# First layer's steady blocks: two steps' first products in one PSUM bank, activations 512 columns wide

## The chip, the cores and the metric

The kernel runs on one core of one Trainium2 chip. The metric is the device time of a whole execution in microseconds. The median before is 1391.65 us over three runs (1391.5 to 1392.34).

## The reference

Three computations run one after the other on 4608 tokens of width 512 (8 batches of 576):

```
attention: chunks of 64 tokens, 8 heads of 64; softmax(q k^T / 8) v within a chunk
first layer:  h = x @ w_in (512 x 2048);  g = h * sigmoid(h);  x = g @ w_out (2048 x 512)
experts:  logits = x @ w_gate + modality_bias[modality_id];  e = argmax
          out = softmax(logits)[e] * (max(x @ w1[e], 0) @ w2[e])   w1[e] 512 x 1024, w2[e] 1024 x 512
```

## The kernel before, in words

Every matrix operand is kept as a high and a low part, and a product is three matmuls: high by high, high by low, low by high. The first layer works on blocks of 256 tokens, `j` = 0 to 17. Blocks 0 and 1 run as a pair while weights are still converted (`order_of`, `g_pair`, lines 136 to 199 and 623 to 644), with activations that are up to 512 columns wide, one half for each block. The change leaves them alone. Blocks 2 to 17 are the steady blocks, the loop from line 1293 on.

A steady block has 16 steps of work, one for each 128 columns of the hidden width, and two more to drain (`NF` = 16, `LAG` = 2). Step `st` does this, in the order in which it is issued:

- `g_parts(j, st - 1)`: ScalarE casts the activation of the step before to its high part (line 653), VectorE subtracts for the low part (line 655).
- Side work: the attention of the next block's two token tiles, router work from a list, woven together by `weave` (one piece of each in turn).
- `g1(j, st)`: the first products, 12 matmuls of 256 columns into one PSUM tile (line 609); then tanh on ScalarE (line 617) and a fused add and multiply on VectorE (line 618), both 256 columns wide. PSUM tile `psh` has two buffers, each one bank of 512 columns; half of a bank is used.
- More side work, then `finish_step(j, st)`: the second products of step `st - 2`, six matmuls of 512 columns into two accumulators (lines 668 to 670). After the last of them the accumulators are copied out, stored, and the block's router work is put on the list.

Each engine runs its instructions in the order of issue. A block has 36 places for side work, two a step. The lists `EVEN` and `ODD` (lines 37 and 38) give, for a block's even and odd attention tile, the places of five pieces: query transpose (VectorE, line 370), scores (TensorE, with maximum, subtract and exponential behind them), normalisation (VectorE), transpose of the probabilities (TensorE), and the product with the values. The key transpose (line 377) comes two places after the query transpose. A negative place lies in the block before. The loads of the next tile are issued by SP with the scores and with the transpose of the probabilities; SP works through its own queue and runs ahead.

Router work: `pump` takes one or two entries of the list a step, first 16 dot products of 512 columns on VectorE (line 690), then `route`, some dozen tiny operations; `pump_late` starts `place` (five tiny matmuls, then small VectorE work and two scatters) one step after `route` at the earliest (`due`, line 1211). In the last block the side places also hold the index gathers and index copies of the first expert tiles (lines 1298 and 1299), their transposes (`trans_x`, lines 1302 and 1303) and the loading and splitting of the first expert's weights.

The expert layer that follows works in stages of two steps: 24 first products of 256 columns (line 1099), each step's relu for itself, then 12 second products of 512 columns (lines 1125 to 1127).

Of the kernel before, what the change touches and what calls it, by code (L numbers as in the profile page):

```python
# [9 lines left out]
F32 = mybir.dt.float32  # L10
# [4 lines left out]
ACTF = mybir.ActivationFunctionType  # L15
ALU = mybir.AluOpType
# [4 lines left out]
P = 128  # L21
# [12 lines left out]
BLK32 = 3  # L34


EVEN = (-12, -8, 5, 9, 15)
ODD = (9, 15, 19, 24, 28)
EVEN0 = (3, 9, 11, 15, 20)
ODD0 = (15, 20, 22, 26, 30)  # L40

# [161 lines left out]
def attention_moe_moe_kernel(  # L203
# [14 lines left out]
    nc = tc.nc  # L218
# [6 lines left out]
    NF = DFF // P  # L225
# [4 lines left out]
    scale = 1.0 / float(D) ** 0.5  # L230

    const = ctx.enter_context(tc.tile_pool(name="const", bufs=1))
    sb = ctx.enter_context(tc.tile_pool(name="sb", bufs=1))
# [29 lines left out]
    def ps_h():  # L263
        return ps.tile([P, 512], F32, tag="h", bufs=2, name="psh")
# [320 lines left out]
    def weave(gens):  # L585

        gens = list(gens)
        while gens:
            gens = [g for g in gens if next(g, weave) is not weave]


    gst = {}

    gps = {}

    def g1(j, f):
        g1_mm(j, f)
        g1_act(j, f)

    def g1_mm(j, f, pair=None):  # L600
        half, fi = divmod(f, 8)
        hi, lo = xT[j]
        hps = ps_h() if pair is None else pair
        n = 0
        for kk in range(KD):
            wh = big1[:, half * 4 + kk, 0, fi * P:(fi + 1) * P]
            wl = big1[:, half * 4 + kk, 1, fi * P:(fi + 1) * P]
            for w, x in ((wh, hi), (wh, lo), (wl, hi)):
                nc.tensor.matmul(hps[:, :256], lhsT=w, rhs=x[:, kk, :], start=n == 0, stop=n == 3 * KD - 1)  # L609
                n += 1  # L610
        if pair is None:
            gps[j, f] = hps

    def g1_act(j, f):
        hps = gps.pop((j, f))
        g = sb.tile([P, 256], F32, tag="g", bufs=3, name="g")
        nc.scalar.activation(out=g, in_=hps[:, :256], func=ACTF.Tanh, scale=0.5)  # L617
        nc.vector.scalar_tensor_tensor(out=g, in0=g, scalar=1.0, in1=hps[:, :256], op0=ALU.add, op1=ALU.mult)  # L618
        gst[j, f] = g

    pair = {}

# [23 lines left out]
    def hid(name, shape):  # L646
        return sb.tile(shape, F32R, tag="hid", bufs=5, name=name)

    def g_parts(j, f):
        g = gst[j, f]  # L650
        gx = hid("g", [P, 2, 256])
        gh, gl = gx[:, 0], gx[:, 1]
        nc.scalar.copy(gh, g)  # L653
        yield
        nc.vector.tensor_tensor(out=gl, in0=g, in1=gh.bitcast(F32), op=ALU.subtract)  # L655
        gst[j, f] = (gh, gl)

    acc = {}

    def g2(j, f):  # L660
        gh, gl = gst.pop((j, f))
        half, fi = divmod(f, 8)
        pc, o = half * 4 + fi // 2, (fi % 2) * 512
        wh, wl = big2[:, pc, 0, o:o + 512], big2[:, pc, 1, o:o + 512]
        for t in range(2):
            c = slice(t * P, (t + 1) * P)
            a = acc[j][t]
            nc.tensor.matmul(a, lhsT=gh[:, c], rhs=wh, start=f == 0, stop=False)  # L668
            nc.tensor.matmul(a, lhsT=gh[:, c], rhs=wl, start=False, stop=False)  # L669
            nc.tensor.matmul(a, lhsT=gl[:, c], rhs=wh, start=False, stop=f == NF - 1)  # L670
# [4 lines left out]
    def x2_evac(j):  # L675
        x2[j] = []
        for t in range(2):
            x = t2("x2t")
            nc.scalar.activation(out=x, in_=acc[j][t], func=ACTF.Copy, scale=0.5)  # L679
            r0 = (2 * j + t) * P  # L680
            nc.sync.dma_start(out=x2d[r0:r0 + P, :], in_=x)
            x2[j].append(x)
        del acc[j]
        if j < NB - 1:
            lg[j] = sb.tile([P, 2, E], F32, tag="lg", bufs=2, name="lg")
# [482 lines left out]
    with tc.manual_schedule():  # L1168
# [3 lines left out]
        def once(fn, *a):  # L1172
            fn(*a)
            return
            yield
# [7 lines left out]
        def att_side(side, t, steps):  # L1183
            fns = (att_Tq, att_S, att_norm, att_PT32, att_PV32)
            side[steps[0] + 2].append(lambda: att_Tk(t))
            for fn, f in zip(fns, steps):
                one = fn in (att_Tq, att_PT32)
                side[f].append((lambda fn=fn: once(fn, t)) if one else (lambda fn=fn: fn(t)))
            if t + 1 < NTILE:
                side[steps[1]].append(lambda: once(load_qk, t + 1))  # L1190
                side[steps[3]].append(lambda: once(load_nat, t + 1, "v"))

        rq = []
        now, due = [0], [0]

        def push_router(j):
            for i in range(2 * E):
                rq.append(("d", lambda i=i: once(dot, j, i)))
            rq.append(("r", lambda: route(j)))
            rq.append(("p", lambda: place(j, *pend.pop(j))))  # L1200
            if j == NB - 3:
                rq.append(("r", choose_first))

        def pump(n):
            out = []
            while wg and rq and n > 0 and rq[0][0] != "p":
                kind, fn = rq.pop(0)
                out.append(fn())
                n -= 1
                if kind != "d":  # L1210
                    due[0] = now[0] + 1
                    break
            return out

        def pump_late():
            if rq and rq[0][0] == "p" and now[0] >= due[0]:
                g = rq.pop(0)[1]()
                next(g)
                return [g]
            return []  # L1220

        def finish_step(j, st):
            f = st - LAG
            if 0 <= f < NF:
                if f == 0:
                    mk = ps_att if j == 1 else ps_acc
                    acc[j] = [mk(), mk()]
                g2(j, f)
                if f == NF - 1:
                    x2_evac(j)  # L1230
                    if j < NB - 1:
                        push_router(j)
# [4 lines left out]
        for n, idle in todo:  # L1237
            what = n[0]
            hps = None
            if what == "g1":  # L1240
                st = n[2] + n[1] * SKEW
# [3 lines left out]
                hps = gps[st][:, n[1] * 256:(n[1] + 1) * 256]  # L1245
# [16 lines left out]
            if n == ("lo", NF - 1):  # L1262
# [7 lines left out]
                    out=wgb.rearrange("p e d -> p (e d)"),  # L1270
                    in_=wgt_d.rearrange("(o e) d -> o (e d)", o=1).to_broadcast([P, E * DM]),
# [14 lines left out]
        late_gens = []  # L1286
        nsteps = NF + LAG
        sides = {i: [] for i in range(2 * nsteps * (NB - 2))}
        for t in range(2 * BLK32, NTILE):
            base = 2 * nsteps * (t // 2 - BLK32)  # L1290
            steps = (ODD if base else ODD0) if t % 2 else (EVEN if base else EVEN0)
            att_side(sides, t, [base + i for i in steps])
        for j in range(2, NB):
            last = j == NB - 1
            side = {i: sides.pop(2 * nsteps * (j - 2) + i) for i in range(2 * nsteps)}
            if last:
                for i in range(2 * FIXED):
                    side[8].append(lambda i=i: once(gather_id, i))
                    side[12].append(lambda i=i: once(make_oid, i))
                side[14].append(lambda: once(gather, 0))  # L1300
                side[14].append(lambda: once(gather, 1))
                side[26].append(lambda: once(trans_x, 0))
                side[30].append(lambda: once(trans_x, 1))
                for n in range(8):
                    i, h = divmod(n, 2)
                    side[(8, 9, 16, 17, 20, 21, 24, 25)[n]].append(lambda i=i, h=h: once(load_first, i, h))
                    f1, f2 = ((8, 10), (9, 11), (12, 13), (14, 15))[i]
                    side[2 * f1 + h].append(lambda i=i, h=h: split_first(i, 0, h))
                    side[2 * f2 + h].append(lambda i=i, h=h: split_first(i, 1, h))
            for st in range(nsteps):  # L1310
                now[0] += 1
                gens = [g_parts(j, st - 1)] if 1 <= st <= NF else []
                gens += [fn() for fn in side[2 * st]] + late_gens
                if j > 2 or st > 1:
                    gens += pump(2 if last or len(rq) > 16 else 1)
                weave(gens)
                if st < NF:
                    g1(j, st)
                weave([fn() for fn in side[2 * st + 1]])
                finish_step(j, st)  # L1320
                late_gens = pump_late()
        assert not rq
        j = NB - 1

# [76 lines left out]
        last = 2 * LONE  # L1401
# [95 lines left out]
```

## Time and profile before

| | |
|---|---|
| median of three runs | 1391.65 us |
| the profiled execution | 1393.78 us |
| its span, first to last instruction | 1392.0 us |
| mean granted clock of TensorE over the span | 0.995 |
| busy: TensorE, VectorE, ScalarE, GpSimd | 98%, 69%, 44%, 12% |
| steady blocks | from 137.4 us to 941.4 us |

In the profile PE is TensorE's matmul, PEld its weight loads, DVE VectorE, ACT ScalarE, POOL GpSimd and SP SyncE, which issues DMAs. A matmul's start is recorded and its end is modelled, so the distance from start to start says how fast the stream runs. A part in square brackets at the end of a timeline row is the idle time before that instruction and what released it. Granted clock 1.00 is the full 2.4 GHz.

### The profile page before, as it was taken

What the parts mean: (1) busy time and instruction counts of PE and PEld (TensorE: products, weight loads), DVE (VectorE), ACT (ScalarE), POOL (GpSimd) and SP (SyncE); (2) the same over time, 40 slices, a digit from 0 to 9 for tenths busy, and PEclk for the clock granted to TensorE, in tenths of its full rate; (3) what the DMA queues carried; (4) which work ended last, traced back from release to release, by engine and by line L of the source; (5) the groups of instructions that cost most, each with busy time, mean ns of one, the idle gap of its engine ahead of it and who ended that gap; (6) DMA issues with size and microseconds to landing.
All of it is one profiled execution on the core that took longest, in us unless ns stands there. A gap on an engine that the chain in (4) does not pass through costs nothing. (4 is left out here: it accounts for less than half of the span.)

```text
span 1392.0 us, 26469 instructions
## 1 busy us (share of the span) xinstructions
PE 1368.0 (98%) x9755; PEld 1226.0 (88%) x9755; DVE 967.3 (69%) x2370; ACT 606.5 (44%) x1234; POOL 160.4 (12%) x173
## 2 busy tenths in 40 slices
PE   8899999999999999999999999999999999999997
PEld 7788888988898888898898888889889989989996
DVE  5997986776777677677677767674677666666664
ACT  5554333333333333333333333352555555555553
POOL 0000000000000000000000000022223222232311
PEclk9899999999999999999999999999999999999999
DMA  9555421221131132132132120231777767776662
GB/s 214 167 177 162 102 51 35 39 59 35 31 62 31 32 62 43 20 61 50 27 47 57 32 35 24 69 85 47 245 251 217 230 208 236 212 230 223 229 208 75
DMA packets 242394, 153.81 MB, mean 110 GB/s; under 512 B 189474, under 2 KB 189510, under 8 KB 242128
## 3 DMA queue, kind: packets, MB, share of 16 engines
q1 hardware_dynamic: 234000, 133.07, 36.3%
q0 software_dynamic: 8256, 18.96, 3.7%
q8 instruction: 79, 1.29, 0.4%
q14 instruction: 59, 0.48, 0.1%
HBM read 132.48 MB, written 20.01 MB: 110 GB/s over the span
## 5 line engine op out<-in xcount | busy, mean ns | idle before, releaser
L609 PE MATMUL psh<-xh,big 128*128 128x256 f32 x2304 | 456.1, 283 | 0.0
L609 PEld LDWEIGHTS psh<-xh,big 128*128 128x128 f32 x2304 | 372.0, 189 | 12.3 <-issue 2.7
L609 PE MATMUL psh<-xl,big 128*128 128x256 f32 x1152 | 324.4, 282 | 0.1
L609 PEld LDWEIGHTS psh<-xl,big 128*128 128x128 f32 x1152 | 217.6, 189 | 9.3 <-DVE xl L526 0.3
L1099 PE MATMUL psh<-xgh,big 128*128 128x256 f32 x1152 | 217.5, 282 | 1.1 <-DVE h L1109 1.0
L618 DVE SCALAR_TENSOR_TENSOR g<-g,psh 128x256 f32<-128x256 f32 x256 | 107.1, 418 | 143.4 <-ACT g L617 140.6
L668 PE MATMUL psc<-big,g 128*128 128x512 f32 x512 | 204.7, 400 | 0.0
L670 PE MATMUL psc<-big,g 128*128 128x512 f32 x512 | 202.1, 395 | 1.3 <-DVE g L655 1.3
L669 PE MATMUL psc<-big,g 128*128 128x512 f32 x512 | 202.1, 395 | 0.0
L690 DVE CUSTOM_DVE_ANT_0 dump<-x2t,wgb 128x512 bf16<-128x512 f32 x272 | 184.9, 680 | 8.2 <-ACT x2t L679 6.3
L617 ACT ACTIVATE g<-psh 128x256 f32<-128x256 f32 x256 | 98.0, 383 | 211.0 <-PE psh L609 196.8
L1099 PEld LDWEIGHTS psh<-xgh,big 128*128 128x128 f32 x1152 | 181.7, 189 | 5.1 <-DVE h L1109 1.4
L653 ACT CAST g<-g 128x256 fp32r<-128x256 f32 x256 | 103.9, 406 | 153.4 <-DVE g L618 148.5
L1099 PE MATMUL psh<-xgl,big 128*128 128x256 f32 x576 | 161.9, 281 | 0.2 <-DVE xgl L1090 0.2
L1109 DVE SCALAR_TENSOR_TENSOR h<-psh,h 128x256 fp32r<-128x256 f32 x144 | 60.7, 423 | 127.2 <-ACT h L1108 118.2
L1108 ACT ACTIVATE h<-psh 128x256 fp32r<-128x256 f32 x144 | 55.2, 384 | 189.0 <-PE psh L1099 164.6
L787 POOL DMA_INDIRECT perm<-rpg,rdi x36 | 36.8, 1022 | 764.5 <-DVE rdi L786 638.7
L655 DVE TENSOR_TENSOR g<-g 128x256 fp32r<-128x256 f32 x256 | 107.7, 421 | 18.1 <-ACT g L653 18.1
L670 PEld LDWEIGHTS psc<-big,g 128*128 128x128 f32 x512 | 96.0, 188 | 23.8 <-DVE g L655 1.7
L1099 PEld LDWEIGHTS psh<-xgl,big 128*128 128x128 f32 x576 | 108.7, 189 | 3.8 <-DVE xgl L1090 0.5
L668 PEld LDWEIGHTS psc<-big,g 128*128 128x128 f32 x512 | 96.6, 189 | 14.9 <-ACT xh L445 2.4
L669 PEld LDWEIGHTS psc<-big,g 128*128 128x128 f32 x512 | 96.2, 188 | 12.5
(252 smaller groups left out, 2042.8 us busy)
## 6 DMA issues: line engine op xcount, KB each, us to landing
rb<-in_moe_w_dram SPq DMA_DIRECT2D x144, 256.0 KB
wr<-in_moe_w_dram SPq DMA_DIRECT2D x68, 512.0 KB
x2d<-x2t SPq DMA_DIRECT2D x36, 256.0 KB
ra<-in_moe_w_in_dram SPq DMA_DIRECT2D x8, 1024.0 KB
rb<-in_moe_w_out_dram SPq DMA_DIRECT2D x8, 1024.0 KB
qk<-in_q_dram SPq DMA_DIRECT2D x240, 32.0 KB
qk<-in_k_dram SPq DMA_DIRECT2D x240, 32.0 KB
vn<-in_v_dram SPq DMA_DIRECT2D x28, 256.0 KB
```

The costliest lines, as they stand in the source:

```text
L609: nc.tensor.matmul(hps[:, :256], lhsT=w, rhs=x[:, kk, :], start=n == 0, stop=n == 3 * KD - 1)
L617: nc.scalar.activation(out=g, in_=hps[:, :256], func=ACTF.Tanh, scale=0.5)
L618: nc.vector.scalar_tensor_tensor(out=g, in0=g, scalar=1.0, in1=hps[:, :256], op0=ALU.add, op1=ALU.mult)
L653: nc.scalar.copy(gh, g)
L655: nc.vector.tensor_tensor(out=gl, in0=g, in1=gh.bitcast(F32), op=ALU.subtract)
L668: nc.tensor.matmul(a, lhsT=gh[:, c], rhs=wh, start=f == 0, stop=False)
L669: nc.tensor.matmul(a, lhsT=gh[:, c], rhs=wl, start=False, stop=False)
L670: nc.tensor.matmul(a, lhsT=gl[:, c], rhs=wh, start=False, stop=f == NF - 1)
L690: nc.vector.tensor_tensor_reduce(out=dump, in0=x2[j][t], in1=wg[0][:, e, :], scale=1.0, scalar=0.0, op0=ALU.mult, op1=ALU.add, accum_out=l ...
L1099: nc.tensor.matmul(hp[:, :256], lhsT=w[:, part, :], rhs=x[:, :, kk * P:(kk + 1) * P], start=i == 0, stop=i == 3 * KD - 1,)
L1108: nc.scalar.activation(out=gh, in_=hp[:, :256], func=ACTF.Relu)
L1109: nc.vector.scalar_tensor_tensor(out=gl, in0=hp[:, :256], scalar=0.0, in1=gh.bitcast(F32), op0=ALU.max, op1=ALU.subtract)
```

## The change

Two steps become one stage `d`. In its first half: side work, the 12 first products of step 2d into the left half of a bank, side work, the 12 of step 2d+1 into the right half, then one tanh and one fused multiply over all 512 columns. In its second half: one cast and one subtract of 512 columns (`g_parts(j, d)`, issued in the same stage as the first products), side work, the second products of step 2d-2, side work, those of step 2d-1. Ninth stage: only the second products of steps 14 and 15. The 36 places are kept, four a stage. The high and low parts are now two tiles of 512 columns instead of the halves of one. Even tiles' query transposes move from place -12 to -15, the normalisations one place earlier, and `place` waits one step longer after `route`.

```diff
-EVEN = (-12, -8, 5, 9, 15)
-ODD = (9, 15, 19, 24, 28)
+EVEN = (-15, -8, 4, 9, 15)
+ODD = (9, 15, 18, 24, 28)
...
+    def g1_stage(j, d, side):
+
+        hps = ps_h()
+        g1_mm(j, 2 * d, hps[:, :256])
+        weave(side)
+        g1_mm(j, 2 * d + 1, hps[:, 256:])
+        pair["g", d] = g = sb.tile([P, 512], F32, tag="g", bufs=3, name="g")
+        nc.scalar.activation(out=g, in_=hps, func=ACTF.Tanh, scale=0.5)
+        nc.vector.scalar_tensor_tensor(out=g, in0=g, scalar=1.0, in1=hps, op0=ALU.add, op1=ALU.mult)
+
+    def g_parts(j, d):
+        g = pair.pop(("g", d))
+        gh, gl = hid("gh", [P, 512]), hid("gl", [P, 512])
+        nc.scalar.copy(gh, g)
         yield
         nc.vector.tensor_tensor(out=gl, in0=g, in1=gh.bitcast(F32), op=ALU.subtract)
-        gst[j, f] = (gh, gl)
+        for n in range(2):
+            gst[j, 2 * d + n] = (gh[:, n * 256:(n + 1) * 256], gl[:, n * 256:(n + 1) * 256])
...
-                    due[0] = now[0] + 1
+                    due[0] = now[0] + 2
...
-            for st in range(nsteps):
-                now[0] += 1
-                gens = [g_parts(j, st - 1)] if 1 <= st <= NF else []
-                gens += [fn() for fn in side[2 * st]] + late_gens
-                if j > 2 or st > 1:
-                    gens += pump(2 if last or len(rq) > 16 else 1)
-                weave(gens)
-                if st < NF:
-                    g1(j, st)
-                weave([fn() for fn in side[2 * st + 1]])
-                finish_step(j, st)
-                late_gens = pump_late()
+            for d in range(nsteps // 2):
+                for half in range(2):
+                    now[0] += 1
+                    gens = [g_parts(j, d)] if half and d < NF // 2 else []
+                    gens += [fn() for fn in side[4 * d + 2 * half]] + late_gens
+                    if j > 2 or d > 0:
+                        gens += pump(2 if last or len(rq) > 16 else 1)
+                    weave(gens)
+                    between = [fn() for fn in side[4 * d + 2 * half + 1]]
+                    if not half and d < NF // 2:
+                        g1_stage(j, d, between)
+                    elif not half:
+                        weave(between)
+                    else:
+                        finish_step(j, 2 * d)
+                        weave(between)
+                        finish_step(j, 2 * d + 1)
+                    late_gens = pump_late()
```

## Rows read from the trace of the kernel before

**Rows 1.** page, part 1, whole span: busy us (share) xinstructions:
```profile
PE 1368.0 (98%) x9755; PEld 1226.0 (88%) x9755; DVE 967.3 (69%) x2370; ACT 606.5 (44%) x1234; POOL 160.4 (12%) x173
```

**Rows 2.** windows of one block's length: stretch, length, busy us and count by engine, clock:
```profile
139.00:189.20 50.20, 50.16 (x370) 44.03 (x369) 44.02 (x123) 17.82 (x43) 2.12 (x2) 1.00 0.33 72
390.00:440.20 50.20, 50.20 (x371) 44.84 (x370) 35.89 (x105) 18.51 (x43) 1.92 (x2) 1.00 0.22 43
892.00:942.20 50.20, 48.89 (x317) 43.71 (x316) 36.71 (x108) 24.02 (x55) 10.82 (x10) 1.00 0.41 106
```

**Rows 3.** timeline, TensorE, first and first after two plain steps: start us, us, engine, line:
```profile
416.10 0.28 PE L609 MATMUL psh<-xh,big 128*128 128x256 f32 x1
...
421.73 0.28 PE L609 MATMUL psh<-xh,big 128*128 128x256 f32 x1
```

**Rows 4.** timeline, TensorE, two stages of the expert layer:
```profile
1157.98 0.28 PE L1099 MATMUL psh<-xgh,big 128*128 128x256 f32 x1
...
1160.83 0.40 PE L1125 MATMUL psc<-big,h 128*128 128x512 f32 x1
...
1163.63 0.28 PE L1099 MATMUL psh<-xgh,big 128*128 128x256 f32 x1
...
1169.27 0.28 PE L1099 MATMUL psh<-xgh,big 128*128 128x256 f32 x1
```

**Rows 5.** groups by line and shape, steady blocks: busy us, mean ns | idle:
```profile
L655 DVE TENSOR_TENSOR g<-g 128x256 fp32r<-128x256 f32 x256 | 107.7, 421 | 18.1 <-ACT g L653 18.1
L618 DVE SCALAR_TENSOR_TENSOR g<-g,psh 128x256 f32<-128x256 f32 x255 | 106.7, 418 | 139.9 <-ACT g L617 137.1
L653 ACT CAST g<-g 128x256 fp32r<-128x256 f32 x256 | 103.9, 406 | 153.4 <-DVE g L618 148.5 <-DVE g L655 4.4
L617 ACT ACTIVATE g<-psh 128x256 f32<-128x256 f32 x255 | 97.6, 383 | 210.1 <-PE psh L609 195.9 <-issue 9.1 <-PE psa L771 0.9
```

**Rows 6.** groups by line and shape, the paired blocks before them:
```profile
L641 DVE TENSOR_TENSOR gpl<-gp,gph 128x512 fp32r<-128x512 f32 x14 | 9.6, 684 | 0.7 <-ACT gph L638 0.7
L633 DVE SCALAR_TENSOR_TENSOR gp<-gp,psh 128x512 f32<-128x512 f32 x14 | 9.5, 678 | 0.0
...
L638 ACT CAST gph<-gp 128x512 fp32r<-128x512 f32 x14 | 8.6, 613 | 0.8 <-DVE gp L633 0.8
L629 ACT ACTIVATE gp<-psh 128x512 f32<-128x512 f32 x14 | 8.3, 594 | 3.2 <-PE psh L609 3.2
```

**Rows 7.** timeline, all engines, hand-overs after one step's first products:
```profile
404.05 0.29 PE L609 MATMUL psh<-xh,big 128*128 128x256 f32 x1
...
404.44 0.38 ACT L617 ACTIVATE g<-psh 128x256 f32<-128x256 f32 x1 [1.28 <-PE psh L609]
...
404.85 0.42 DVE L618 SCALAR_TENSOR_TENSOR g<-g,psh 128x256 f32<-128x256 f32 x1 [1.24 <-ACT g L617]
```

**Rows 8.** timeline, all engines, the late low half in the last block:
```profile
912.04 0.15 DVE L1067 CAST oi<-idg 128x1 uint32<-128x1 f32 x1 [1.09 <-DMA idg<-perm,gidx]
...
912.22 0.40 PE L669 MATMUL psc<-big,g 128*128 128x512 f32 x1
...
913.45 0.42 DVE L655 TENSOR_TENSOR g<-g 128x256 fp32r<-128x256 f32 x1
...
913.93 0.50 PE L670 MATMUL psc<-big,g 128*128 128x512 f32 x1 [1.31 <-DVE g L655]
...
914.26 0.39 PE L668 MATMUL psc<-big,g 128*128 128x512 f32 x1
```

**Rows 9.** timelines of SP and VectorE, the even tile: last of its loads, its first reader:
```profile
400.20 2.00 SPq L359 DMA_DIRECT2D qk<-in_k_dram  x4
...
424.17 0.70 DVE L370 STREAM_TRANSPOSE qT<-qk 128x512 f32<-128x512 f32 x1
```

**Rows 10.** timeline, all engines, second gathered tile, last block:
```profile
935.95 0.59 ACT L1089 CAST xgh<-psa 128x512 fp32r<-128x512 f32 x1 [0.49 <-PE psa L1088]
...
936.57 0.69 DVE L1090 TENSOR_TENSOR xgl<-psa,xgh 128x512 fp32r<-128x512 f32 x1 [0.76 <-ACT xgh L1089]
```

More of the change, by code (lines that the diff above doesn't have):

```diff
@@ L594, in attention_moe_moe_kernel, with g1_mm @@
     gps = {}
[L596 to L600, printed above, removed]
+    def g1_mm(j, f, hps):
         half, fi = divmod(f, 8)
         hi, lo = xT[j]
-        hps = ps_h() if pair is None else pair
         n = 0
@@ L610, in g1_mm @@
                 n += 1
[L611 to L619, printed above, removed]
     pair = {}
@@ L647, in hid @@
         return sb.tile(shape, F32R, tag="hid", bufs=5, name=name)
[L649 to L652, printed above, removed]
+    def g1_stage(j, d, side):
[9 more added lines that the diff above has]
+        gh, gl = hid("gh", [P, 512]), hid("gl", [P, 512])
         nc.scalar.copy(gh, g)
```

## The prediction

> **What bounds the kernel now.** I read the page's busy shares first, then windows of one block's length, then TensorE's timeline, because a change that touches three engines is worth only what the engine that sets the end gets from it. TensorE is busy 1368.0 of 1392.0 us, VectorE 967.3, ScalarE 606.5 [rows 1]. By windows it is sharper: in a middle block TensorE is busy 50.20 of 50.20 us at a granted clock of 1.00 (2.4 GHz), VectorE 35.9 and ScalarE 18.5; even in the first steady block, VectorE's fullest, TensorE has 50.16 [rows 2]. Only the last block falls short, 48.89, and 1.31 us of that is one wait, a second product waiting for VectorE's low half [rows 2, 8]. So in 16 steady blocks nothing but TensorE's own stream sets the time, except in that one place.
>
> Busy is not peak, so I read the stream by its starts. Two plain steps (12 first products of 256 columns, 6 second products of 512, twice) take from 416.10 to 421.73, 5.63 us [rows 3]. The Trainium skill (Perfetto Trace Analysis, Identifying the Most-Contended Engine) warns that matmul occupancy is no measure of the distance to the roofline. Here weight loads are busy 44.84 of 50.20, 89% [rows 2], so by that rule some headroom could exist; this counts below only as a rival.
>
> **What the change takes away, adds and moves.** *TensorE's stream.* No matmul goes or comes: each stage still has 24 first and 12 second products. Only the order changes, from 12+6+12+6 to 24+12. The trace has that order already: the expert layer's stages run 24 products of 256 columns and 12 of 512, same shapes. Two such stages without anything between take 1157.98 to 1169.27, 5.645 us each [rows 4]. Against 5.63 that is +0.015 us a stage. A block has eight stages; in two of them attention's matmuls stand inside or at the edge and break the stream in either order, so I count six: 0.09 us a block, 16 blocks, **+1.4 us**. Bounds: 0, if the difference belongs to the experts' operands; and 0.02 (5.65, the slower of the two stages, less 5.63) times eight times 16, +2.6.
>
> *ScalarE and VectorE.* Per stage, two tanh (383 ns), two fused multiplies (418), two casts (406) and two subtracts (421) become one each of 594, 678, 613 and 684 ns, taken from the paired blocks' 512-column forms [rows 5, 6]. ScalarE saves 2x(383+406)-(594+613) = 371 ns a stage, VectorE 2x(418+421)-(678+684) = 316 ns; 128 stages make 47 and 40 us of engine time. I cost both at **0**: neither engine is what TensorE waits for, by the full windows [rows 2].
>
> *The dependent chain.* This is the price of the width: the low half must be there before its second product. In mid-block the deadline is a whole stage later and the chain has more than 2 us to spare. The tight place is the block's end, where no first products follow. Count from the start of the last first product of stage 7. Tanh starts 0.39 later, VectorE 0.03 after tanh ends [rows 7]; so 0.39+0.594+0.03 = 1.01, multiply to 1.69, cast to 2.34, subtract to 3.06 with a 0.03 hand-over each [rows 6, 7]. Meanwhile TensorE runs one more 0.12 spacing, 12 second products at 0.233 (1160.83 to 1163.63 holds 12) [rows 4] and two more, and starts the first product of the low half at 3.38. A late one also stretches the next spacing by 0.1 (913.93 to 914.26 is 0.33) [rows 8], so 3.28 counts. 3.06 is in time by 0.2, where the narrow chain, by the same count with the narrow durations, had 1.2: **0**. Router work stands behind the subtract in VectorE's queue, and a router dot there runs while ScalarE casts. Bounds: 0, and the chain starting behind one more dot (about 0.65 us, the 0.69 of a wide operation less its overlap) in each of 16 blocks: 0.43 late, +6.9. I take 0, since the durations are those of the same chain in the paired blocks.
>
> Here the Trainium skill speaks against the change: Perfetto Trace Analysis, Matmuls, wants independent groups to rotate through PSUM banks so that the evacuation of one overlaps the next. Sharing a bank takes that overlap from the first step of each stage. By the rows it has slack to lose; by the rule it is the first rival below.
>
> *Moved attention and router work.* For even tiles the query transpose comes three half-steps earlier, about 4 us. Its last load was issued by 402.2, its first reader ran at 424.17 [rows 9], so 18 us of cover remain; SP's queue order does not change. The key transpose stands still behind the score products that read its single buffer. The two normalisations come one half-step earlier, VectorE work with more than a step of cover. Placing waits one step longer and lands at the block boundary: five tiny matmuls either way, 0. PSUM and hidden buffers get no scarcer (two banks per two stages instead of per two steps; two 512-wide halves a stage, five buffers). Bounds for these together: -0.5 to +1.
>
> *The last block.* In the old order VectorE stands behind index copies that wait for a DMA, the last at 912.04, then two dots, and the low half of step 5 ends at 913.87; its second product, due at 912.45, starts at 913.93 [rows 8]. From 912.22 to 914.26 is 2.04 where two spacings of 0.233 are due: 1.57 us lost. In the new order those copies stand at a stage's start, behind the subtract that the next second products need, and the delayed stage has until after 24 further first products. It fits by about 0.3 us. **-1.6**. If not, the wait stays smaller: -1.6 to 0. New in that block: the second gathered tile's transposes now stand between stage 7's cast and subtract; its cast of 0.59 and subtract of 0.69 [rows 10] run in front of the low half: 2.34+0.59+0.69+0.68, less some 0.1 of overlap, is 4.2, against 3.28 plus 0.44 for the four transposes = 3.72 (my estimate: 128 columns each, half of a 256-column spacing of 0.119, and a stretched spacing of 0.1 at either side [rows 4, 8]). Late by 0.5: **+0.5** (0 to 1).
>
> *Sum.* +1.4 - 1.6 + 0.5 = +0.3 us. The profiled execution took 1393.78 (span 1392.0 and 1.78 around it) and would go to 1394.1; the median of the runs is 1391.65, 2.1 below it, so I forecast **1392.0**.
>
> **Rivals.** *1. The chain decides at the block's end (slower).* From the point where the low half comes later than 3.28 us after the last first product, every block pays. With one dot in front of the multiply in every block that is the 6.9 above, 1398.6; in half of the blocks 1395.1. For it: the slack falls from 1.2 to a fifth of a microsecond. Against it: by the order of issue no router dot falls due just before that multiply, and attention's VectorE work there ends before the last first products do.
>
> *2. The early block overloads VectorE (a little slower).* In the first steady block VectorE is busy 44.0 of 50.2 [rows 2] with two dots a step, and now the four dots of a stage stand together with one wide chain. If two stages there miss by 0.7 us: +1.4 more, 1393.5. Against: the change frees 8 x 0.316 = 2.5 us of VectorE in that block.
>
> *3. Fewer, wider instructions help TensorE (faster).* If 24+12 costs nothing and the tile in the last block doesn't delay: -1.6, 1390.0. To pass 0.2% TensorE's spacing itself must shrink, for which only the weight loads' 89% speaks [rows 2]; 1% of the 45 us of plain stages in each block would be -7, 1384.5. Against: the expert stages have the same order and no shorter spacing [rows 4].
>
> **Chances.** A measurement of this kernel can tell about 0.2%, 2.8 us, from no change. Forecast 0.60, rival 1 0.15, rival 2 0.10, rival 3 in its small form 0.08 and with shorter spacing 0.07. So faster 0.07, same 0.77 (forecast, small form of rival 3, most of rival 2), slower 0.16 (rival 1 and a bad case of rival 2). The range runs from 1389.6, just under the small form of rival 3, to 1395.6, over rival 1 in half of the blocks; outside it are the full rival 1 and the shorter spacing.
>
> **What would show it.** Right: TensorE busy 50.2 of 50.2 in a middle block; plain stages of 5.64 to 5.65; 128 wide tanh near 594 ns; no 1.3 us wait at step 5 of the last block, and a wait of about half a microsecond before the second product of its stage 7. Wrong: waits of TensorE for the low half at block ends (rival 1), between 140 and 190 us (rival 2), or stages under 5.6 us (rival 3).

## The result, and the profile after

The changed kernel takes 1401.56 us (median of four runs, 1400.25 to 1403.39) where the kernel before, on the same chip, takes 1391.99 (1391.5 to 1392.93). The ratio is 1.0069, interval 1.0051 to 1.0086: slower, by more than the 0.2% that a measurement can tell, and above the range of the forecast. The profiled execution took 1400.89, with a span of 1399.1 against 1392.0: 7.1 us to find in the two traces. (The medians differ by 9.6: the kernel before's profiled execution was 1.8 above its median, the changed kernel's 0.7 below.)

The page of the changed kernel, part 1 (busy us, share of the span, instructions; compare [rows 1]):
```profile
PE 1371.7 (98%) x9755; PEld 1227.1 (88%) x9755; DVE 949.0 (68%) x2114; ACT 564.6 (40%) x978; POOL 160.3 (11%) x173
```
Exactly the promised instructions are gone, 256 on VectorE and 256 on ScalarE, and both engines are busy for less time, by 18 and 42 us. (By the groups of [rows 5] and those below, the operations themselves save 38 and 45; VectorE's records overlap their neighbours', so its busy time falls by less.) The groups by line and shape of the changed kernel give the four wide operations, each at the price taken from [rows 6] within 8 ns:
```profile
L650 DVE TENSOR_TENSOR gl<-g,gh 128x512 fp32r<-128x512 f32 x128 | 88.4, 691 | 18.4 <-ACT gh L648 13.1
L643 DVE SCALAR_TENSOR_TENSOR g<-g,psh 128x512 f32<-128x512 f32 x128 | 87.7, 685 | 176.0 <-ACT g L642 175.7
...
L648 ACT CAST gh<-g 128x512 fp32r<-128x512 f32 x128 | 79.5, 621 | 135.7 <-DVE g L643 126.9 <-DVE lg L686 8.8
...
L642 ACT ACTIVATE g<-psh 128x512 f32<-128x512 f32 x128 | 76.6, 598 | 226.8 <-PE psh L604 219.4 <-issue 6.8 <-ACT dp L431 0.6
```
Where is the time, then? The windows of a block's length, of the changed kernel, answer to [rows 2] (stretch, length, busy us and count of PE, PEld, DVE, ACT and POOL, granted clock, DMA share, GB/s):
```profile
139.00:189.00 50.00, 49.64 (x367) 43.72 (x366) 41.69 (x104) 14.83 (x26) 2.40 (x2) 1.00 0.35 74
390.00:440.00 50.00, 50.00 (x365) 44.78 (x364) 33.91 (x85) 15.83 (x27) 2.17 (x2) 1.00 0.22 43
892.00:942.00 50.00, 45.05 (x289) 39.98 (x288) 32.20 (x99) 16.79 (x33) 8.56 (x8) 0.97 0.44 106
```
A middle block is still full. In the last window almost 5 us of TensorE are missing, where 1.31 were before, and the granted clock is 0.97 there: not a slower stream everywhere but a hole in one place. The copies of the accumulators at a block's end date the blocks. ScalarE's timeline, kernel before (end of block 2, which is the first steady one; end of block 16, where the last begins; end of the last):
```profile
188.90 1.30 ACT L679 ACTIVATE x2t<-psc 128x512 f32<-128x512 f32 x2 [2.15 <-PE psc L670]
...
893.14 1.30 ACT L679 ACTIVATE x2t<-psc 128x512 f32<-128x512 f32 x2 [2.37 <-PE psc L670]
...
940.86 1.30 ACT L679 ACTIVATE x2t<-psc 128x512 f32<-128x512 f32 x2 [1.90 <-PE psc L670]
```
and the changed kernel, the same three places:
```profile
189.69 1.30 ACT L675 ACTIVATE x2t<-psc 128x512 f32<-128x512 f32 x2 [3.59 <-PE psc L666]
...
894.87 1.30 ACT L675 ACTIVATE x2t<-psc 128x512 f32<-128x512 f32 x2 [0.64 <-PE psc L666]
...
950.39 1.24 ACT L675 ACTIVATE x2t<-psc 128x512 f32<-128x512 f32 x2 [2.33 <-PE psc L666]
```
Up to the last block 1.73 us are lost; in the last block 55.52 us pass instead of 47.72, +7.80; from there to the end of the span 448.7 instead of 451.1, -2.43. The sum is +7.10.

What TensorE waits for at the second products of the changed kernel's steady blocks, from the view of waits (total, times, longest); the first row holds a wait of 4.52 and one of 0.58, the second one of 0.43 and one of 1.08, all in the last block:
```profile
PE psc L664 <- ACT gh L648: 5.1, 2, 4.5
PE psc L666 <- DVE gl L650: 1.5, 2, 1.1
```
The chain behind the wait of 4.5 is read backwards, in the timeline of all engines of the changed kernel:
```profile
917.12 0.15 DVE L1063 CAST oi<-idg 128x1 uint32<-128x1 f32 x1 [6.66 <-issue]
...
920.11 0.15 DVE L1063 CAST oi<-idg 128x1 uint32<-128x1 f32 x1 [1.12 <-DMA idg<-perm,gidx]
920.18 0.68 DVE L686 CUSTOM_DVE_ANT_0 dump<-x2t,wgb 128x512 bf16<-128x512 f32 x1
...
920.90 0.69 DVE L686 CUSTOM_DVE_ANT_0 dump<-x2t,wgb 128x512 bf16<-128x512 f32 x1
...
921.52 0.68 DVE L643 SCALAR_TENSOR_TENSOR g<-g,psh 128x512 f32<-128x512 f32 x1
...
922.24 0.62 ACT L648 CAST gh<-g 128x512 fp32r<-128x512 f32 x1 [8.79 <-DVE lg L686]
...
922.91 0.50 PE L664 MATMUL psc<-big,gh 128*128 128x512 f32 x1 [4.52 <-ACT gh L648]
...
923.47 0.69 DVE L650 TENSOR_TENSOR gl<-g,gh 128x512 fp32r<-128x512 f32 x1
...
924.21 0.80 PE L666 MATMUL psc<-big,gl 128*128 128x512 f32 x1 [0.43 <-DVE gl L650]
```
TensorE waits for the cast, the cast for the multiply (its row names a dot, but it reads what the multiply writes, and that ends at 922.20), and the multiply stands in VectorE's queue behind four index copies and two dots. The copies wait for the index gathers; VectorE does nothing for 6.66 us ahead of the first of them. That row says "issue" and names no one; the next copies name the gather. Why are the gathers late? GpSimd's timeline of the changed kernel:
```profile
902.46 0.96 POOL L783 DMA_INDIRECT perm<-rpg,rdi  x1 [39.36 <-DVE gf L855]
908.65 1.30 POOL L783 DMA_INDIRECT perm<-rpg,rdi  x1 [5.24 <-DVE g L643]
913.89 0.98 POOL L1056 DMA_INDIRECT idg<-perm,gidx  x1 [3.94 <-DMA perm<-rpg,rdi]
```
and of the kernel before:
```profile
892.40 0.96 POOL L787 DMA_INDIRECT perm<-rpg,rdi  x1 [39.81 <-DVE gf L859]
897.15 1.19 POOL L787 DMA_INDIRECT perm<-rpg,rdi  x1 [3.79 <-DVE lg L690]
905.47 1.37 POOL L1060 DMA_INDIRECT idg<-perm,gidx  x1 [7.13 <-DVE lg L690]
```
The gathers stand behind the scatters of the last placed block in GpSimd's queue and read what these write; in the changed kernel the row of the first gather names the scatter's data, in the kernel before a dot. The scatters moved from 892.40 to 902.46, relative to the last block's start from 0.7 before it to 7.6 after it, and the gathers with them. The placing that feeds them, on TensorE's timeline, in the kernel before:
```profile
890.63 0.18 PE L767 MATMUL psa<-rob,triu 128*128 128x8 bf16 x1
```
and in the changed one:
```profile
898.22 0.18 PE L763 MATMUL psa<-rob,triu 128*128 128x8 bf16 x1
```
It used to come before a block's end and now comes in the next block. The last block is only where this hurts: the place of block 8, too, stands 1.1 us before the end of block 9 in the kernel before, and 6.2 us after it in the changed one.

The router list explains the offset. A block puts 18 entries on it (16 dots, route, place) and has 18 steps to take them off. One entry a step goes, two while more than 16 are left; a place holds up everything behind it until it is due. When it is due one step after its route, 18 entries take 18 steps, and the list keeps the distance to which it has once caught up. With two steps they take 19. One step a block must then be made up by a doubled one, and that happens only while more than 16 entries are left, so the list runs with a longer backlog for good: by the code's own count a block's place comes in the 21st step after its entries, in place of the 17th, and in the traces 56.6 us in place of 49.2 (block 8: from the block's end at 492.70 to 549.29, and from 491.21 to 540.44).

After the wait, the clock. Windows of 1 us of the changed kernel, same columns as above:
```profile
922.00:923.00 1.00, 0.09 (x1) 0.09 (x1) 0.96 (x4) 0.76 (x2) 0.00 (x0) 1.00 0.68 82
923.00:924.00 1.00, 0.78 (x2) 0.20 (x2) 1.00 (x3) 1.00 (x3) 0.00 (x0) 0.67 0.77 291
924.00:925.00 1.00, 0.79 (x2) 0.70 (x3) 0.96 (x4) 0.39 (x1) 0.00 (x0) 0.50 0.40 152
925.00:926.00 1.00, 1.00 (x4) 0.80 (x3) 1.00 (x3) 0.00 (x0) 0.00 (x0) 0.50 0.00 0
926.00:927.00 1.00, 1.00 (x4) 0.79 (x3) 1.00 (x3) 0.00 (x0) 0.00 (x0) 0.62 0.00 0
```
TensorE had waited 4.5 us; just after it resumed, the granted clock fell to 0.50 (1.2 GHz) and came back some 3.5 us later. The four windows lack 0.33+0.50+0.50+0.38 = 1.7 us of full clock. So the wait cost more than its length.

### The profile page after: what moved, and what is told of

The parts are those of the page before. It is cut to its first block, busy times and chain, and to the rows that moved or that the text cites. A ratio compares the mean times of both kernels' runs of the same rounds, so it can differ in the third digit from the quotient of the medians.

```text
span 1399.1 us, 25653 instructions
## 1 busy us (share of the span) xinstructions
PE 1371.7 (98%) x9755; PEld 1227.1 (88%) x9755; DVE 949.0 (68%) x2114; ACT 564.6 (40%) x978; POOL 160.3 (11%) x173
## 5 line engine op out<-in xcount | busy, mean ns | idle before, releaser
L604 PE MATMUL psh<-xh,big 128*128 128x256 f32 x2304 | 440.1, 283 | 0.0
L604 PEld LDWEIGHTS psh<-xh,big 128*128 128x128 f32 x2304 | 365.0, 189 | 7.6 <-issue 2.9
L664 PE MATMUL psc<-big,gh 128*128 128x512 f32 x512 | 205.4, 401 | 5.1 <-ACT gh L648 5.1
L643 DVE SCALAR_TENSOR_TENSOR g<-g,psh 128x512 f32<-128x512 f32 x128 | 87.7, 685 | 176.0 <-ACT g L642 175.7
L666 PE MATMUL psc<-big,gl 128*128 128x512 f32 x512 | 203.0, 396 | 1.7 <-DVE gl L650 1.5
L665 PE MATMUL psc<-big,gh 128*128 128x512 f32 x512 | 203.2, 397 | 0.0
L642 ACT ACTIVATE g<-psh 128x512 f32<-128x512 f32 x128 | 76.6, 598 | 226.8 <-PE psh L604 219.4
L648 ACT CAST gh<-g 128x512 fp32r<-128x512 f32 x128 | 79.5, 621 | 135.7 <-DVE g L643 126.9
L666 PEld LDWEIGHTS psc<-big,gl 128*128 128x128 f32 x512 | 96.5, 188 | 26.3 <-DVE gl L650 3.6
L664 PEld LDWEIGHTS psc<-big,gh 128*128 128x128 f32 x512 | 96.4, 188 | 25.7 <-ACT gh L648 5.7
L665 PEld LDWEIGHTS psc<-big,gh 128*128 128x128 f32 x512 | 96.5, 188 | 17.3
L650 DVE TENSOR_TENSOR gl<-g,gh 128x512 fp32r<-128x512 f32 x128 | 88.4, 691 | 18.4 <-ACT gh L648 13.1
```

Source lines behind the costliest of these rows:

```text
L642: nc.scalar.activation(out=g, in_=hps, func=ACTF.Tanh, scale=0.5)
```

## The experiments

Theory A is the list that falls behind, caused by `due` alone. Its rivals look for the loss in the wider chain (B) and in the rest of the rearrangement, the moved places among it (C). The first four kernels ran on one chip beside the kernel before (1393.25 us, 1391.63 to 1396.88), the last three on another (1394.72 us, 1392.51 to 1397.38).

**The list kept short, in the changed kernel.**
```diff
-                        gens += pump(2 if last or len(rq) > 16 else 1)
+                        gens += pump(2 if last or len(rq) > 13 else 1)
```


> The changed kernel, with one number changed: a step takes two router entries while more than 13 wait (16 in the changed kernel), so that a block's router work is off the list before the next block's comes; placing still waits two steps. Theory A (the longer wait before placing makes the router list fall a whole block behind, so the last block's scatters, gathers and index copies come 8 us late and VectorE stands behind them): the 4.5 us wait of TensorE in the last block goes, the clock stays at 1.00 there, time 1391.5 to 1395. Theory B (the wait comes of the wide activation itself, which stands behind the index copies whenever they come): 1399 to 1404, wait of 3 us or more still there. Theory C (the earlier places of attention's pieces cost the time): 1399 to 1404.

Measured: 1396.08 us (1394.85 to 1398.09), ratio 1.002 (1.001 to 1.003), just above the range of A. The last block takes 47.21 us at a granted clock of 1.00, and of the waits there one of 0.2 us is left: A has its wait of 4.5 us. But from block 6 on ten blocks take 50.73 to 50.99 us, where the changed kernel had 50.37 to 50.39. The view of waits finds them at the weight loads:
```profile
PEld psc L666 <- DVE gl L650: 7.7, 14, 0.7
```
and this kernel's timeline shows one, at a block's start:
```profile
448.88 0.69 DVE L643 SCALAR_TENSOR_TENSOR g<-g,psh 128x512 f32<-128x512 f32 x1 [2.17 <-ACT g L642]
...
449.49 0.69 DVE L686 CUSTOM_DVE_ANT_0 dump<-x2t,wgb 128x512 bf16<-128x512 f32 x1
...
449.60 0.62 ACT L648 CAST gh<-g 128x512 fp32r<-128x512 f32 x1 [0.76 <-DVE g L643]
...
450.22 0.69 DVE L686 CUSTOM_DVE_ANT_0 dump<-x2t,wgb 128x512 bf16<-128x512 f32 x1
...
450.83 0.69 DVE L650 TENSOR_TENSOR gl<-g,gh 128x512 fp32r<-128x512 f32 x1
...
451.57 0.19 PEld L666 LDWEIGHTS psc<-big,gl 128*128 128x128 f32 x1 [0.54 <-DVE gl L650]
```
Two dots stand between the multiply and the subtract of a block's first stage. The cast is done at 450.22, one dot would be hidden behind it; the second makes the subtract 0.6 late. No second products stand between the first stage's first products and the second's, so the low half is due only 2.85 us and two spacings after the chain began, the same 3.3 us as at the block's end. Those two dots fall there because the list is longest just after a block has put its 18 entries on it. The changed kernel itself has this wait in blocks 3 and 4 (50.76 and 50.75 us), while its list catches up. In block 2 (53.92 us, 53.45 before) it has another: TensorE waits 0.36 us for VectorE's normalisation of the probabilities. The three blocks lose 1.25 of the 1.73 us that go before the last block.

**The longer wait of a place alone, in the kernel before.**
```diff
-                    due[0] = now[0] + 1
+                    due[0] = now[0] + 2
```


> The kernel before, with only the wait before placing made two steps. Theory A: the list falls a block behind here too, the scatters of block 15 come inside the last block, and TensorE waits 3 us or more there: 1396 to 1403. Theories B and C: nothing that they rest on is in this kernel, 1391 to 1393.

Measured: 1402.38 us (1402.04 to 1403.88), ratio 1.0063 (1.0047 to 1.008), the loss of the changed kernel. The last block takes 58.17 us, and TensorE has one wait there:
```profile
PE psc L670 <- DVE g L655: 9.0, 1, 9.0
```
No width, bank or moved attention is in it. One changed constant makes the loss; B and C fall as its main cause. The narrow form even waits longer behind the late index copies than the wide one: the copies run from 916.78 to 920.63, and the subtract of line 655 at 921.89.

**The last block's index copies and row gathers eight places later, in the changed kernel.**
```diff
-                    side[12].append(lambda i=i: once(make_oid, i))
-                side[14].append(lambda: once(gather, 0))
-                side[14].append(lambda: once(gather, 1))
+                    side[20].append(lambda i=i: once(make_oid, i))
+                side[22].append(lambda: once(gather, 0))
+                side[22].append(lambda: once(gather, 1))
```


> The changed kernel with the last block's four index copies at place 20 instead of 12 and the two gathers of rows at 22 instead of 14. The router list lags as in the changed kernel, but VectorE no longer stands behind the copies for 10 us. Theories A and B: the 4.5 us wait goes, 1392.5 to 1396. Theory C: 1399 to 1404. If the clock's fall is a cost of its own after that wait, it goes too, and the gain is more than the 5 us of waiting.

Measured: 1394.55 us (1392.26 to 1396.85), ratio 1.0002 (0.9991 to 1.0012): no difference from the kernel before can be seen, which speaks against C and does not tell A from B. The list still lags, but VectorE no longer meets the copies before their data is there; the last block takes 48.35 us. So the late list costs its time through VectorE's queue and not through the rows themselves, which come in time even eight places later but for 2.9 us of waits for them in the expert layer.

**The attention's old places, in the changed kernel.**
```diff
-EVEN = (-15, -8, 4, 9, 15)
-ODD = (9, 15, 18, 24, 28)
+EVEN = (-12, -8, 5, 9, 15)
+ODD = (9, 15, 19, 24, 28)
```


> The changed kernel with the old lists of places for attention's pieces (query transposes of even tiles at -12, normalisations at 5 and 19). Theories A and B: no difference from the changed kernel, 1399.5 to 1404. Theory C: back to 1391 to 1394.

Measured: 1409.67 us (1408.05 to 1410.06), ratio 1.011 (1.0093 to 1.0127): none of the theories. The middle blocks take 0.4 to 0.5 us more than in the changed kernel, and the waits of TensorE name the place:
```profile
PE psa L389 <- DVE dk L377: 4.0, 14, 1.4
```
The scores wait for the key transposes: 1.4 us in block 2 and 0.2 in each of 13 others, about half of what a middle block loses. In stages the old places are no longer early enough. The move that I priced at nothing is one that the stages need. Without it they lose some 6 us more by the two ratios (1.011 and 1.0069), 9.2 by the two profiled spans.

**The list kept short, and the second dot only ahead of first products.**
```diff
-                        gens += pump(2 if last or len(rq) > 16 else 1)
+                        gens += pump(2 if last or (len(rq) > 12 and not half) else 1)
```


> The kernel after, with the router list kept short by a limit of 12 instead of 16, and its second dot issued only in even steps, that is, ahead of a stage's first products and never in the weave in which the stage's VectorE subtract stands. The list holds the same place as in e1_pace at the end (place of block 15 in step 15 of block 16). Theory A (the late list costs the wait of the last block; two dots ahead of one subtract cost the 0.37 us that every later block of e1_pace paid): no wait over 0.5 us on TensorE in the last block, steady blocks and the first three at 50.4 us, so e1_pace less 15 times 0.37 less 2 times 0.4: 1390 us, a little faster than the kernel before (1393.25 in the last call). Rival D (the second dot costs its time wherever it stands, since VectorE is behind for the whole of a block's first stages): as e1_pace, 1396.

Measured: 1391.56 us (1389.7 to 1393.19) against 1394.72, ratio 0.9977 (0.9967 to 0.9987): faster than the kernel before, by hardly more than the 0.2% that a measurement can tell. Set against the changed kernel's ratio to the same kernel it is 0.991 (0.988 to 0.994 from the ends of both intervals). The steady blocks take 50.35 to 50.38 us but for one of 50.58 (the kernel before has one of 50.57), the first of them 53.30, 50.38 and 50.36, so the 0.37 us a block were the second dot, as A has it and against D. The last block takes 47.20; its waits of TensorE are one:
```profile
PE psc L666 <- DVE gl L650: 0.2, 1, 0.2
```
**A place due after one step again, in the changed kernel.**
```diff
-                    due[0] = now[0] + 2
+                    due[0] = now[0] + 1
```


> The kernel after, with a place due one step after its route as before, instead of two; nothing else. Theory A (the second step of waiting is what makes the list need more than the 18 steps of a block): the list stays level, the wait of 4.5 us in the last block is gone, that block takes 47 to 48.5 us; the blocks up to 6 may keep 0.4 us each where two dots stand ahead of a subtract; 1392.5 to 1394 us. If the place's five matmuls now come before the route's VectorE chain is done, TensorE waits there once a block, up to some 2 us: 1425 at the worst. Rival E (the stages themselves, by their coarser steps, deliver the last scatters late): the wait in the last block stays at several us, 1398 to 1402.

Measured: 1409.64 us (1408.74 to 1410.55), ratio 1.0105 (1.009 to 1.0121). The last block takes 47.21 us, so the lag is gone and E falls. But the bound that the expectation gave for the other case came true in ten blocks of 51.85 to 52.13 us:
```profile
PE psa L763 <- DVE rob L746: 13.8, 10, 1.4
```
The place's first matmul needs the end of route's chain on VectorE. With one step between them, in stages, it stands in TensorE's queue 1.4 us before that is done. So the two steps are needed in stages, and what they lack is a list that can afford them.

**Both in the kernel before: a place due after two steps, and the limit at 12.**
```diff
-                    due[0] = now[0] + 1
+                    due[0] = now[0] + 2
...
-                    gens += pump(2 if last or len(rq) > 16 else 1)
+                    gens += pump(2 if last or len(rq) > 12 else 1)
```


> The kernel before, with a place due two steps after its route as in e2_before_due2, but with the limit of the list at 12 instead of 16, so that the list keeps up. Theory A (it is the lag, not the longer wait of a place in itself): the 9.0 us that TensorE waited in the last block of e2_before_due2 are gone, 1391 to 1395 us (two dots in a step may cost up to 0.4 us a block: 1399). Rival F (a place two steps after its route is late by itself, through the scatters that follow it): 1400 to 1403 as in e2_before_due2.

Measured: 1393.52 us (1392.25 to 1395.9), ratio 0.9995 (0.9986 to 1.0004). The wait of 9.0 us is gone, the last block takes 46.12 us, and F falls: the longer wait of a place costs nothing by itself.

## Why the prediction was wrong

*The step that failed* is this, of the moved router work: "Placing waits one step longer and lands at the block boundary: five tiny matmuls either way, 0." I priced where the matmuls of a place land and not what the place holds up. Behind it in the list stand the next block's dots, and behind its scatters, in GpSimd's queue, the gathers of the last block; the list had no step to spare, so that one step more for each block turned into a standing backlog of four. What that cost is 7.80 us in the last block of the changed kernel; that one constant alone, in the kernel before, cost a ratio of 1.0063, and with the list kept short the same two steps cost nothing (0.9995). Its bounds, -0.5 to +1 us, were drawn from work that moves, and could not contain a queue that falls behind.

*The last block, -1.6 and +0.5.* The sentence "in the new order those copies stand at a stage's start, behind the subtract that the next second products need" was right as an order, but "it fits by about 0.3 us" took the gathers' time from the kernel before. The gathers came 8.4 us later (905.47 and 913.89), and then it was the multiply behind the copies that was late. Where the list is short, the old wait of [rows 8] is gone as forecast and the last block takes 47.20, 0.52 less than before, against a forecast of 1.1 less. But the seventh experiment, with the narrow steps, has lost that wait too, and its last block takes 46.12, 1.6 less. So a short list is enough to remove it, with the gathers starting 7.5 us into the last block (10.7 in the fifth experiment, 12.3 in the kernel before); that the stages' order would do it by itself is not shown. The last block of 55.52 is that 47.20 and 8.3: the four waits there (4.52, 0.43, 0.58 and 1.08, less the 0.22 that stays) make 6.4, the clock 1.7, and 0.2 is left over.

*The second gathered tile, +0.5*, was too small in the changed kernel and too large without the lag. The timeline of the changed kernel in stage 7 has the predicted order:
```profile
945.92 0.62 ACT L648 CAST gh<-g 128x512 fp32r<-128x512 f32 x1 [2.46 <-DVE g L643]
946.44 0.58 ACT L1085 CAST xgh<-psa 128x512 fp32r<-128x512 f32 x1
...
946.59 0.50 PE L664 MATMUL psc<-big,gh 128*128 128x512 f32 x1 [0.58 <-ACT gh L648]
...
947.05 0.69 DVE L1086 TENSOR_TENSOR xgl<-psa,xgh 128x512 fp32r<-128x512 f32 x1 [1.17 <-ACT xgh L1085]
947.66 0.68 DVE L650 TENSOR_TENSOR gl<-g,gh 128x512 fp32r<-128x512 f32 x1
...
948.40 0.50 PE L666 MATMUL psc<-big,gl 128*128 128x512 f32 x1 [1.08 <-DVE gl L650]
```
Its chain began late, though: the multiply ran behind the late place's small operations and the weight splits, and the waits are 0.58 and 1.08. With the short list only 0.22 is left, inside the bounds of 0 to 1.

*TensorE's stream, +1.4.* The mechanism held and the size was too large. The changed kernel's timeline shows one stage (start of 12 second products, of the next 24 first products, of the next second products), 2.79 and 2.85 us:
```profile
417.82 0.39 PE L664 MATMUL psc<-big,gh 128*128 128x512 f32 x1
...
420.61 0.28 PE L604 MATMUL psh<-xh,big 128*128 128x256 f32 x1
...
423.46 0.40 PE L664 MATMUL psc<-big,gh 128*128 128x512 f32 x1
```
That is 5.64, as the expert layer had it [rows 4]. But a whole middle block went from 50.35 to 50.38 only, 0.03 instead of 0.09. Whether the plain stages cost less than 0.015 each or the stages with attention inside gave something back was not separated.

*The chain at the block's end, 0.* Right: middle blocks with a full list show no wait there. But the same deadline of 3.3 us holds at a block's start, which I did not look at; rival 1's mechanism (one dot more in front of the low half) was real there, at 0.37 to 0.4 us a block instead of 0.43, in two blocks of the changed kernel and in nearly all of the first experiment's.

*ScalarE and VectorE, 0.* Right: 60 us of the engines' busy time went (forecast 87), and the steady blocks are no shorter for it. *Moved attention work, 0*: right as it stands; the fourth experiment shows that the move is what makes it so.

*Still open.* From the last block to the end the changed kernel is 2.4 us shorter, the fifth experiment's 2.8. By the waits 2 us of the first are the expert tiles' gathered rows and a first product that waits for VectorE's part of a relu. The kernel before has
```profile
PE psa L1088 <- DMA xrow<-x2d,oi: 2.4, 2, 1.3
...
PE psh L1099 <- DVE h L1109: 1.0, 1, 1.0
```
where the changed kernel has 1.4 of the first and none of the second. These waits differ from kernel to kernel here (0.8 to 3.2 us for the rows), the time from the last block to the end also differs among the kernels with narrow steps (449.0 to 452.3 us), and no experiment isolated them. What the traces do show is where the best version gained: from the copy of block 0's accumulators, at the end of the paired blocks, to the start of the last block it takes 757.8 us, the kernel before 757.7. So the steady blocks that the change rearranged gave nothing, and how much of the 0.23% is the stages themselves stays open.

## What to carry to other kernels

A due time in a hand-made schedule is a capacity: before making an entry wait longer, count the entries a period brings and the steps it has, then follow the last period, where the backlog is paid. Ask of a delayed item what stands behind it in every queue, to the DMAs that read what it writes. And when work is regrouped into stages, check the dependent chain at the first stage of a block as well as at the last, and cap what a scheduler may put between the two halves of that chain.

## What the runs showed of the hardware that I had not expected

TensorE's granted clock fell to 0.50 within 2 us of its return from a wait of 4.5 us, stayed there for two windows of 1 us, and was 1.00 again from 927 on: 1.7 us on top of the wait. In the second experiment it fell while TensorE still waited (9.0 us, from 913.4 to 922.4): windows of 1 us show 0.50 from 918 to 928. The Trainium skill (TensorE: Matmul & The Clock Gate, What's actually happening) says the same in general: the clock knows a lower level of half the rate, and idling brings it back there. The trace agrees, with 0.50 as the lowest window; I had priced waits by their length alone. A gather issued behind a scatter to the same table began 5.2 us after the second scatter did (908.65 to 913.89), with 3.94 us of that spent on the scatter's data; over the nine profiles this distance is 5.2 to 8.3 us. So here one such step cost several microseconds, whoever waited for it.
